# Fourier mixing and a gated convolution network on one Trainium2 core: a third product in the steps where VectorE has side work

## The chip, the cores and the metric

The kernel runs on one core of one Trainium2 chip. The metric is the device time of one execution in microseconds (us). The core's engines run side by side and meet at semaphores: TensorE (PE in the profile), VectorE (DVE), ScalarE (ACT), GpSimd (POOL), and SyncE (SP), whose queue issues most of the transfers.

## The reference

The input is `x`, 8 batches of 3136 x 256 in float32. It is Fourier-transformed along the sequence and the feature axis, and the real part goes into a gated network with 1024 hidden features:

```python
X = np.fft.fft(np.fft.fft(x, axis=1), axis=2).real
h = np.maximum(X @ w_in, 0.0)
conv_out = sum(conv_w[k] * hp[:, k:k + S, :] for k in range(3))   # hp: h padded by one row at each end
out = (h * (1.0 / (1.0 + np.exp(-conv_out)))) @ w_out
```

The code is condensed; the padding is along the sequence.

## The kernel before, in words

The transform along the sequence is done batch by batch. The rows of a batch are loaded as two halves `xh[b, 0]` and `xh[b, 1]`, the mirrored rows by four gathers each on GpSimd's queue (`load_ops`, L131). VectorE folds the rows onto each other: seven operations per half (`fold_ops`, L141 to L208: two `pair`, two `both`, `evens`, two `feats`), some 1.1 to 1.2 us each. TensorE multiplies the folded rows `w` by cosine and sine tables (`units`, PSUM tile `pd`), VectorE combines the parts into `pt` (cosine part) and `qt` (sine part). The feature transform is multiplied into `w_in` beforehand and gives the constant `G`, also of two halves.

The network then goes through 256 steps: 8 batches x 4 chunks of the half sequence x 8 blocks of 128 hidden features. A step computes the hidden rows at position k and at the mirrored position S-k together. Let a be the cosine product (PSUM tile `pa`, first filled by ScalarE's `seed`) and b the sine product (PSUM tile `pb`). The front half of the hidden rows is relu(a + b), the back half relu(a - b). In a step:

- `products` (L680): two fp32 matmuls, `pb` and `pa`; each is two instructions in the profile.
- `copies` (L687): ScalarE copies `pb` into `nb` twice, once with its sign changed (L693).
- `combine` (L695): VectorE adds `pa` and a half of `nb` and clamps at zero, once for the front and once for the back of `h` (L702). It asks for a buffer of `h` first (`row_of`, L674; 4 buffers), where GpSimd zeroes the two end columns in the first chunk of each batch (L678).
- `first_tap` (ScalarE, L707) and `tap` 1 and 2 (VectorE, L712): the convolution with three taps, over 770 or 832 columns.
- `sigmoid` (ScalarE, L725, in two pieces) and `gate`: the multiplication by `h`, half of the columns on GpSimd (L732) and half on VectorE (L733); in a batch's last chunk 64 more columns on GpSimd (L735).
- `mm2` (L737): the product with `w_out`, six tiles of 128 rows into `po`, accumulated over the 8 feature blocks.

The order of the instructions is written out by hand and each engine takes its queue in order. Cycle t of the main loop (L900) issues sigmoid(t-2), products(t+1), copies(t+1), combine(t), seed(t+2), first_tap(t), tap 1 and tap 2 of t-1, gate(t-2) and mm2(t-3). Side work is hung into cycles through the table `side`, under the names "first", "act", "dve", "pool", "load" and "pe". "dve" stands between the two taps. Side work in early cycles: the narrowing of the weights (`shared`: the last of w_in in cycle 0, w_out in cycles 2, 3, 5 and 7; L543 to L561), the feature column of all batches (`Feature`: `place` in cycle 5, L418 to L431, a VectorE stage in cycles 15 and 32), and the fold of batch 1 in cycles 9 to 19, with two operations in cycles 9, 12 and 16. The fold of batch 2 lies in cycles 20 to 35, and the products of batch 1's transform (`units`) in cycles 20 to 29. The transform of a batch runs through the steps of the batch before it.

Of the kernel before, what the change touches and what calls it, by code (L numbers as in the profile page):

```python
# [12 lines left out]
AF = mybir.ActivationFunctionType  # L13
# [19 lines left out]
BIG = 3.4028234663852886e38  # L33
# [3 lines left out]
def kernel(  # L37
# [10 lines left out]
    nc = tc.nc  # L48
    B, S, D = x.shape
    F = moe_w_in.shape[1]  # L50
    P = 128
# [9 lines left out]
    NF = F // P  # L61
# [27 lines left out]
    act = nc.scalar.activation  # L89

    def mm(o, l, r, start, stop):
        nc.tensor.matmul(o, l, r, start=start, stop=stop, skip_group_check=True)  # L92
# [16 lines left out]
    def load_ops(b, h, eng, other=None, held=False):  # L109


        def plain():
            t = xp.tile([P, 8, 2, D], F32, name="xh", tag="xh")
            xh[b, h] = t
            if held:

                nc.gpsimd.memset(t[0:1, 0, 0, 0:1], 0.0)
            eng.dma_start(out=t[0:NP, 0:4], in_=bass.AP(
                tensor=x.tensor, offset=x.offset + (b * S + 1 + 2 * h) * D,
                ap=[[HQ * D, NP], [Q4 * D, 4], [1, 2 * D]]))  # L120

        def zero():
            t = xh[b, h]
            for s0, n, r in ((0, 4, 0), (4, 3, 1), (7, 1, 0)):
                (other or eng).dma_start(out=t[NP:KR, s0:s0 + n], in_=bass.AP(
                    tensor=x.tensor, offset=x.offset + (b * S + r * Q4) * D,
                    ap=[[D, 1], [Q4 * D, n], [0, 2], [1, D]]))

        def mirrored(m):
            def f():  # L130
                nc.gpsimd.indirect_dma_start(  # L131
                    out=xh[b, h][0:NP, 7 - m].rearrange("p q d -> p (q d)"),
                    out_offset=None,
                    in_=bass.AP(tensor=x.tensor, offset=x.offset,
                                ap=[[2 * D, B * S // 2], [1, 2 * D]]),
                    in_offset=bass.IndirectOffsetOnAxis(ap=idx[0:NP, 0:1], axis=0),
                    element_offset=(b * S + (4 - m) * Q4 - HO + 2 * (1 - h)) * D)
            return f
        return [plain] + [zero] * h + [mirrored(m) for m in range(4)]
# [73 lines left out]
    PQ, eb, er = {}, {}, {}  # L213
# [416 lines left out]
    G = const.tile([P, 2, F], F32, name="G")  # L630
# [29 lines left out]
    hs, gs, pa, pb, po, nb = {}, {}, {}, {}, {}, {}  # L660

    def cut(s):
        b, c, f = s
        ch = chunks[c]
        return ch, ch.k1 - ch.k0, slice(f * P, (f + 1) * P)

    def seed(s):
# [3 lines left out]
        pa[s] = psa.tile([P, 512], F32, name="pa", tag="pa")  # L671
        act(pa[s][:, 0:n], eb[b, c], AF.Copy, scale=ge[:, f:f + 1])  # L672

    def row_of(s):  # L674
        hs[s] = hp.tile([P, HW], F32, name="h", tag="h")
        w = chunks[s[1]].w
        if chunks[s[1]].zeros:
            nc.gpsimd.memset(hs[s][:, 0:w:w - 1], 0.0)  # L678

    def products(s):  # L680
        b, c, f = s
        ch, n, fs = cut(s)
        pb[s] = psb.tile([P, 512], F32, name="pb", tag="pb")
        mm(pb[s][:, 0:n], G[0:P - 1, 1, fs], PQ[b][1][0:P - 1, ch.k0:ch.k1], True, True)
        mm(pa[s][:, 0:n], G[:, 0, fs], PQ[b][0][:, ch.k0:ch.k1], False, True)

    def copies(s):  # L687

        ch, n, fs = cut(s)
        p = pb.pop(s)  # L690
        nb[s] = nbp.tile([P, 2, HN], F32, name="nb", tag="nb")
        for i, cols in enumerate((ch.fcols, ch.cols)):
            act(nb[s][:, i, cols], p[:, cols], AF.Copy, scale=-1.0 if i else 1.0)  # L693

    def combine(s):  # L695

        ch, n, fs = cut(s)
        a, c = pa.pop(s), nb.pop(s)
        row_of(s)
        h = hs[s]  # L700
        for i, (to, cols) in enumerate(((h[:, ch.front], ch.fcols), (h[:, ch.back][:, ::-1], ch.cols))):
            nc.vector._custom_dve(TENSOR_ADD_SAT, out=to, in0=a[:, cols], in1=c[:, i, cols], s0=BIG, s1=0.0)  # L702

    def first_tap(s):
        n = chunks[s[1]].w - 2
# [7 lines left out]

    def shares(s):

        ch = chunks[s[1]]
        w = ch.w - 2
        n = ch.rest[0] if ch.last else w
        return slice(0, n // 2), slice(n // 2, n), slice(n, w)

    def sigmoid(s):

        v, p, r = shares(s)
        for c in (slice(p.start, r.stop), v):
            act(gs[s][:, c], gs[s][:, c], AF.Sigmoid)  # L725

    def gate(s):

        b, c, f = s
        g, h = gs[s], hs.pop(s)[:, 1:]  # L730
        v, p, r = shares(s)
        gt(g[:, p], g[:, p], h[:, p], op=ALU.mult)  # L732
        vt(g[:, v], g[:, v], h[:, v], op=ALU.mult)  # L733
        if r.start < r.stop:
            gt(left[:, f, b % 2 * LEFT:(b % 2 + 1) * LEFT], g[:, r], h[:, r], op=ALU.mult)  # L735
# [69 lines left out]
    n = chunks[0].k1  # L805
    p = psd.tile([P, 512], F32, name="pd", tag="pd")
# [8 lines left out]
    steps = [(b, c, f) for b in range(B) for c in range(len(chunks)) for f in range(NF)]  # L815
    per = len(chunks) * NF
    side = {}

    def at(cycle, where, fn):
        side.setdefault((cycle, where), []).append(fn)  # L820
# [6 lines left out]
    def shared(cycle, w, c):  # L827
        for where, fn in zip(("first", "dve"), w.parts(c, c + 2, room)):
            at(cycle, where, fn)

    shared(0, w_in[3], 0)
    for cycle, c in ((2, 0), (3, 2), (5, 4), (7, 6)):
        shared(cycle, w_out, c)
    for j, fn in enumerate(load_ops(1, 1, nc.sync)):
        at(NF + 1 + j // 3, "load", fn)

    ends = [9, 20, per + 4] + [per * (b - 1) - 3 for b in range(3, B)]
    taken = set()  # L840

    def free(cycle):

        while cycle in taken:
            cycle += 1
        taken.add(cycle)
        return cycle
# [13 lines left out]
    for b in range(1, B):  # L861
        begin, us, *_ = units(b)
        us = us[0:4] + us[5:]
        c0, n = ends[b], per * b - 3 - ends[b]
        at(max(c0, per * (b - 1) + 1), "pe", begin)
        cs = [c0 + i * n // len(us) for i in range(len(us) + 1)]
# [10 lines left out]
    for b in range(1, B):  # L877
        ops, singles = fold_ops(b)
        c0, n = ends[b - 1], ends[b] - ends[b - 1]
        cs = [free(c0 + j * n // len(ops)) if b > 1 else c0 + j * n // len(ops) for j in range(len(ops))]  # L880
        assert cs[-1] < ends[b] and (b > 1 or cs[7] > NF + 3)
        if b + 1 < B:
            for h in range(2):
                for j, fn in enumerate(load_ops(b + 1, h, nc.sync)):
                    at(cs[7 * h + 6] + 1 + j, "load", fn)
        for j, fn in enumerate(ops):
            at(cs[j], "dve", fn)
        for j, fn in singles.items():
            at(cs[j], "pool", fn)
# [4 lines left out]
    n = len(steps)  # L894
    seed(steps[0])
    seed(steps[1])
    products(steps[0])
    copies(steps[0])
    column(1)
    for t in range(n + LAG):  # L900
        def run(where):
            for fn in side.get((t, where), []):
                fn()
        if 0 <= t - 2 < n:
            sigmoid(steps[t - 2])
        run("first")
        if t + 1 < n:
            products(steps[t + 1])
            copies(steps[t + 1])
        run("act")  # L910
        if t < n:
            combine(steps[t])
        if t + 2 < n:
            seed(steps[t + 2])
        if t < n:
            first_tap(steps[t])

        if 0 <= t - 1 < n:
            tap(steps[t - 1], 1)
        run("dve")  # L920
        if 0 <= t - 1 < n:
            tap(steps[t - 1], 2)
        if 0 <= t - 2 < n:
            gate(steps[t - 2])
        run("pool")
        run("load")
        if t >= LAG:
            mm2(steps[t - LAG])
        run("pe")
# [66 lines left out]
```

## Time and profile before

The median of three runs is 1196.29 us (1195.91 to 1196.37).

| engine | busy us | share of the 1195.3 us span |
|---|---|---|
| TensorE (PE) | 1156.0 | 97% |
| VectorE (DVE) | 1135.0 | 95% |
| ScalarE (ACT) | 878.4 | 73% |
| GpSimd (POOL) | 477.5 | 40% |

The chain that ended last, which follows each instruction back to what released it, is 86% TensorE, 5% VectorE and 3% GpSimd. The share of all matmul time that goes to `po` is the largest (706.9 us), the taps (L712) are VectorE's largest group (580.1 us).

How to read the profile: a group's line gives its source line, engine, operation, output and inputs, the count, then busy time and the mean of one, then the time that the engine sat idle just before these instructions and what ended it. A line of the waits says who waited for whom, for how many us in total, how often, and the longest one. A line of the timeline gives the start in us, the length, the instruction, and in brackets the idle time before it. Neighbouring instructions of an engine overlap by about 0.1 us, so the distance from start to start is what one costs.

### The profile page before, as it was taken

The numbers are of one execution on the slowest core, as the hardware profiler recorded it, in microseconds if no ns is written. First come the engines' busy times: TensorE is split into PE (matmuls) and PEld (weight loads), VectorE is DVE, ScalarE is ACT, GpSimd is POOL, SyncE is SP. The second block draws the span as 40 slices with busy tenths as digits, with TensorE's granted clock in tenths as the row PEclk, the third lists the DMA queues.
The fourth block names the chain that finished last, engine by engine and source line by source line (L and its number), as shares of the span: only waits on it lengthen the run. The fifth ranks groups of instructions, "written<-read, shape, count | busy, mean of one in ns | idle before, by whom it ended". The sixth has DMA issues, their size and how long they took to land.

```text
span 1195.3 us, 15307 instructions
## 1 busy us (share of the span) xinstructions
PE 1156.0 (97%) x4802; PEld 888.5 (74%) x4802; DVE 1135.0 (95%) x1642; ACT 878.4 (73%) x1824; POOL 477.5 (40%) x540
## 2 busy tenths in 40 slices
PE   4988999999999999999999999999999999999998
PEld 2655677678777777777777777777777777777776
DVE  7899999999999999999999999999998998999996
ACT  2577666677777877777777777787776777788884
POOL 5225646454273342624345243632224232442224
PEclk9899999999999999999999999999999999999999
DMA  9802243211031210202021020310000100110000
GB/s 231 187 8 82 80 50 103 68 54 61 21 95 45 68 41 22 87 27 81 27 86 53 14 68 27 95 41 27 27 23 32 32 27 27 47 34 28 27 27 31
DMA packets 70067, 66.07 MB, mean 55 GB/s; under 512 B 28107, under 2 KB 57683, under 8 KB 69987
## 3 DMA queue, kind: packets, MB, share of 16 engines
q1 hardware_dynamic: 64349, 51.98, 15.3%
q0 software_dynamic: 5120, 12.85, 3.6%
q8 instruction: 38, 0.62, 0.2%
q10 hardware_dynamic: 518, 0.28, 0.1%
q14 instruction: 42, 0.34, 0.1%
HBM read 39.33 MB, written 25.74 MB: 54 GB/s over the span
## 4 chain that ended last, share of the span: by engine, by line
PE 86%; DVE 5%; issue 3%; POOL 3%; ACT 2%; DMA 0%; ACTq 0%; POOLq 0%; DVEq 0%; SPq 0%
PE po L92 53%; PE pb L92 13%; PE pa L92 13%; PE pd L92 7%; DVE g L712 2%; POOL xh L131 1%; DVE h L702 1%; DVE g L733 1%; ACT nb L693 0%; ACT os L752 0%; ACT g L725 0%; POOL left L735 0%; POOL g L732 0%; DVE w L194 0%; ACT pa L672 0%
## 5 line engine op out<-in xcount | busy, mean ns | idle before, releaser
L92 PE MATMUL po<-wout,g 128*128 128x256 f32 x3072 | 706.9, 380 | 16.8 <-DVE g L733 16.7
L92 PEld LDWEIGHTS po<-wout,g 128*128 128x128 f32 x3072 | 580.3, 190 | 164.2 <-DVE g L733 31.2
L712 DVE SCALAR_TENSOR_TENSOR g<-h,cw,g 128x770 f32<-128x770 f32 (+1 forms) x512 | 580.1, 1133 | 6.2 <-ACT g L707 2.2
L732 POOL TENSOR_TENSOR g<-g,h 128x385 f32<-128x385 f32 (+1 forms) x256 | 276.2, 1079 | 673.0 <-ACT g L725 471.1
L693 ACT ACTIVATE nb<-pb 128x386 f32<-128x386 f32 (+3 forms) x512 | 227.3, 498 | 183.9 <-PE pb L92 183.5
L725 ACT ACTIVATE g<-g 128x385 f32<-128x385 f32 (+2 forms) x512 | 244.3, 529 | 82.9 <-DVE g L712 82.0
L702 DVE CUSTOM_DVE_ANT_0 h<-pa,nb 128x386 f32<-128x386 f32 (+3 forms) x512 | 264.1, 556 | 7.4 <-POOL h L678 6.5
L707 ACT ACTIVATE g<-h,cw 128x770 f32<-128x770 f32 (+1 forms) x256 | 243.9, 953 | 0.0
L92 PE MATMUL pb<-qt,G 127*128 127x387 f32 (+2 forms) x512 | 214.4, 500 | 0.9 <-ACT G L641 0.9
L92 PE MATMUL pa<-pt,G 128*128 128x387 f32 (+2 forms) x512 | 211.8, 494 | 0.0
L672 ACT ACTIVATE pa<-eb,ge 128x387 f32<-128x387 f32 (+2 forms) x256 | 154.2, 603 | 2.5 <-DVE h L702 1.9
L92 PEld LDWEIGHTS pa<-pt,G 128*128 128x128 f32 x512 | 97.1, 190 | 73.8 <-issue 19.1
L733 DVE TENSOR_TENSOR g<-g,h 128x385 f32<-128x385 f32 (+1 forms) x256 | 147.4, 576 | 2.2 <-ACT g L725 2.2
L92 PE MATMUL pd<-tab,w 98*128 98x196 f32 (+3 forms) x448 | 118.4, 356 | 0.0
L131 POOL DMA_INDIRECT xh<-in_x_dram,idx x64 | 106.9, 1671 | 13.3 <-issue 10.8
L92 PEld LDWEIGHTS pb<-qt,G 127*128 127x128 f32 x512 | 91.2, 190 | 19.3 <-ACT G L641 2.0
L92 PEld LDWEIGHTS pd<-tab,w 98*128 98x128 f32 (+1 forms) x448 | 83.7, 191 | 12.3
L735 POOL TENSOR_TENSOR left<-g,h 128x64 f32<-128x64 f32 x64 | 63.8, 997 | 0.0
L752 ACT COPY os<-po 128x256 f32<-128x256 f32 x196 | 57.5, 389 | 8.0 <-PE po L92 4.7
L156 DVE TENSOR_TENSOR xh<-xh 98x1020 f32<-98x1020 f32 (+1 forms) x32 | 39.4, 1237 | 2.9 <-DMA xh<-in_x_dram,idx 2.9
L167 DVE TENSOR_TENSOR xh<-xh 98x1024 f32<-98x1024 f32 (+1 forms) x32 | 38.9, 1216 | 0.1
L178 POOL COPY w<-xh 98x4 f32<-98x4 f32 (+1 forms) x32 | 20.6, 644 | 6.1 <-DVE xh L167 3.6
(120 smaller groups left out, 316.5 us busy)
## 6 DMA issues: line engine op xcount, KB each, us to landing
out_dram<-os SPq DMA_DIRECT2D x192, 128.0 KB
xh<-in_x_dram SPq DMA_DIRECT2D x16, 784.0 KB
eb<-ed SPq DMA_DIRECT2D x16, 193.5 KB
tab<-dft_seq_dram SPq DMA_DIRECT2D x4, 589.5 KB
raw<-in_moe_w_in_dram SPq DMA_DIRECT2D x4, 512.0 KB
raw<-in_moe_w_out_dram SPq DMA_DIRECT2D x1, 2048.0 KB
eb<-ed SPq DMA_DIRECT2D x8, 209.0 KB
eb<-ed SPq DMA_DIRECT2D x7, 193.0 KB
```

What stands on the lines that cost most here:

```text
L92: nc.tensor.matmul(o, l, r, start=start, stop=stop, skip_group_check=True)
L131: nc.gpsimd.indirect_dma_start(out=xh[b, h][0:NP, 7 - m].rearrange("p q d -> p (q d)"), out_offset=None, in_=bass.AP(tensor=x.tensor, offs ...
L672: act(pa[s][:, 0:n], eb[b, c], AF.Copy, scale=ge[:, f:f + 1])
L693: act(nb[s][:, i, cols], p[:, cols], AF.Copy, scale=-1.0 if i else 1.0)
L702: nc.vector._custom_dve(TENSOR_ADD_SAT, out=to, in0=a[:, cols], in1=c[:, i, cols], s0=BIG, s1=0.0)
L707: act(gs[s], hs[s][:, 0:n], AF.Copy, scale=cw[:, 0, s[2]:s[2] + 1])
L712: stt(out=g, in0=h[:, k:k + n], scalar=cw[:, k, f:f + 1], in1=g, op0=ALU.mult, op1=ALU.add)
L725: act(gs[s][:, c], gs[s][:, c], AF.Sigmoid)
L732: gt(g[:, p], g[:, p], h[:, p], op=ALU.mult)
L733: vt(g[:, v], g[:, v], h[:, v], op=ALU.mult)
L735: gt(left[:, f, b % 2 * LEFT:(b % 2 + 1) * LEFT], g[:, r], h[:, r], op=ALU.mult)
L752: nc.scalar.copy(out=osb[:, j % 2], in_=pt[:, j % 2])
```

## The change

The change adds a third matmul to a step in which VectorE has side work: `pa` also accumulates the sine product, so it holds a + b, and ScalarE writes the front half of `h` as Relu of `pa` in place of a copy. The back half is still made by VectorE, from `pa` and -2b, since (a + b) - 2b = a - b. VectorE is left with one combine of the two. The test is `third(i)`: steps 3 to 19 and 30 to 35 with an entry under "dve". In a cycle with such a step the gate under way is split anew: three quarters on VectorE and a quarter on GpSimd. `row_of` is called a cycle earlier for these steps, in `copies`. Batch 1's fold starts in cycle 4 and has one operation in each cycle that is not taken by narrowing or the feature stage: cycles 4, 6, 8 to 14 and 16 to 20. The four gathers of batch 1's second half are issued one a cycle, in cycles 9 to 12, and not one in cycle 9 and three in cycle 10. The purpose is to take load off VectorE in these cycles and to make it even.

```diff
+    def triple(s):
+        return third(steps.index(s))
+
+    def third(i):
+        return (3 <= i < ends[1] or per - 2 <= i < ends[2]) and (i, "dve") in side
...
-        mm(pa[s][:, 0:n], G[:, 0, fs], PQ[b][0][:, ch.k0:ch.k1], False, True)
+        mm(pa[s][:, 0:n], G[:, 0, fs], PQ[b][0][:, ch.k0:ch.k1], False, not triple(s))
+        if triple(s):
+            mm(pa[s][:, 0:n], G[0:P - 1, 1, fs], PQ[b][1][0:P - 1, ch.k0:ch.k1], False, True)
...
-        for i, cols in enumerate((ch.fcols, ch.cols)):
-            act(nb[s][:, i, cols], p[:, cols], AF.Copy, scale=-1.0 if i else 1.0)
+        if triple(s):
+            act(nb[s][:, 1, ch.cols], p[:, ch.cols], AF.Copy, scale=-2.0)
+            row_of(s)
+            act(hs[s][:, ch.front], pa[s][:, ch.fcols], AF.Relu)
+        else:
+            for i, cols in enumerate((ch.fcols, ch.cols)):
+                act(nb[s][:, i, cols], p[:, cols], AF.Copy, scale=-1.0 if i else 1.0)
...
-        row_of(s)
+        if not triple(s):
+            row_of(s)
...
-            nc.vector._custom_dve(TENSOR_ADD_SAT, out=to, in0=a[:, cols], in1=c[:, i, cols], s0=BIG, s1=0.0)
+            if i or not triple(s):
+                nc.vector._custom_dve(TENSOR_ADD_SAT, out=to, in0=a[:, cols], in1=c[:, i, cols],
+                                      s0=BIG, s1=0.0)
...
-        return slice(0, n // 2), slice(n // 2, n), slice(n, w)
+        m = n - n // (4 if third(steps.index(s) + 2) else 2)
+        return slice(0, m), slice(m, n), slice(n, w)
...
-        at(NF + 1 + j // 3, "load", fn)
+        at(NF + 1 + max(j - 2, 0), "load", fn)
...
-        cs = [free(c0 + j * n // len(ops)) if b > 1 else c0 + j * n // len(ops) for j in range(len(ops))]
+        if b == 1:
+            cs = [c for c in range(4, ends[1] + 1) if c not in taken]
+            assert len(cs) == len(ops) and cs[7] > NF + 4
+        else:
+            cs = [free(c0 + j * n // len(ops)) for j in range(len(ops))]
```

The cycles of the w_out narrowing are entered in `taken` as well, so that the fold leaves them out.

More of the change, by code (lines that the diff above doesn't have):

```diff
@@ L817 @@
     side = {}
+    taken = set()
     def at(cycle, where, fn):
@@ L833 @@
         shared(cycle, w_out, c)
+        taken.add(cycle)
     for j, fn in enumerate(load_ops(1, 1, nc.sync)):
-        at(NF + 1 + j // 3, "load", fn)
+        at(NF + 1 + max(j - 2, 0), "load", fn)
     ends = [9, 20, per + 4] + [per * (b - 1) - 3 for b in range(3, B)]
-    taken = set()
     def free(cycle):
@@ L879 @@
         c0, n = ends[b - 1], ends[b] - ends[b - 1]
-        cs = [free(c0 + j * n // len(ops)) if b > 1 else c0 + j * n // len(ops) for j in range(len(ops))]
-        assert cs[-1] < ends[b] and (b > 1 or cs[7] > NF + 3)
+        if b == 1:
[3 more added lines that the diff above has]
+            cs = [free(c0 + j * n // len(ops)) for j in range(len(ops))]
+            assert cs[-1] < ends[b]
         if b + 1 < B:
```

## The prediction

> **What bounds the kernel now.** I read the page first: engines, groups, then the waits, then busy time by stretch. Engines and three groups:
>
> ```profile
> PE 1156.0 (97%) x4802; PEld 888.5 (74%) x4802; DVE 1135.0 (95%) x1642; ACT 878.4 (73%) x1824; POOL 477.5 (40%) x540
> ...
> L92 PE MATMUL po<-wout,g 128*128 128x256 f32 x3072 | 706.9, 380 | 16.8 <-DVE g L733 16.7
> L732 POOL TENSOR_TENSOR g<-g,h 128x385 f32<-128x385 f32 (+1 forms) x256 | 276.2, 1079 | 673.0 <-ACT g L725 471.1
> L702 DVE CUSTOM_DVE_ANT_0 h<-pa,nb 128x386 f32<-128x386 f32 (+3 forms) x512 | 264.1, 556 | 7.4 <-POOL h L678 6.5
> ```
>
> TensorE and VectorE are nearly equally loaded. TensorE waits in the step loop only for VectorE's gate (L733), 16.7 us in all. Which cycles? The waits between 63.75 and 150 us put nearly all of it there:
>
> ```profile
> PE po L92 <- DVE g L733: 13.9, 15, 2.8
> ```
>
> The same view for 196 to 246 us has 2.8 us in five waits. Busy time by stretch, cut where VectorE starts cycles 3, 9, 20, 30 and 36 (columns: stretch, length, then busy time and instructions of PE, PEld, DVE, ACT, POOL):
>
> ```profile
> 63.94:93.15 29.21, 23.63 (x94) 17.44 (x94) 27.70 (x47) 19.95 (x40) 6.57 (x17) 1.00 0.13 35
> 93.15:149.75 56.60, 48.75 (x193) 33.93 (x191) 56.53 (x81) 39.44 (x100) 33.07 (x25) 1.00 0.23 72
> 149.75:202.62 52.87, 52.59 (x224) 40.53 (x224) 52.06 (x82) 34.70 (x71) 24.71 (x27) 1.00 0.43 85
> 202.62:232.44 29.82, 27.35 (x112) 19.20 (x112) 28.77 (x41) 20.60 (x44) 18.84 (x21) 1.00 0.15 43
> ```
>
> Cycles 3 to 19 and 30 to 35 are bound by VectorE, the rest by TensorE. Only there can the change gain, and there it adds TensorE work.
>
> Last, VectorE's timeline in cycle 12 and GpSimd's near 146 us:
>
> ```profile
> 107.19 0.55 DVE L733 TENSOR_TENSOR g<-g,h 128x385 f32<-128x385 f32 x1
> 107.66 1.02 DVE L702 CUSTOM_DVE_ANT_0 h<-pa,nb 128x386 f32<-128x386 f32 x2
> 108.59 2.70 DVE L712 SCALAR_TENSOR_TENSOR g<-h,cw,g 128x770 f32<-128x770 f32 x1
> 111.22 1.21 DVE L167 TENSOR_TENSOR xh<-xh 98x1024 f32<-98x1024 f32 x1
> ```
>
> ```profile
> 146.30 4.25 POOL L732 TENSOR_TENSOR g<-g,h 128x385 f32<-128x385 f32 x1 [2.67 <-issue]
> ```
>
> A tap normally takes 1.01 us; here it took 2.70, while GpSimd, released by a long gather, ran two gate multiplies. The other way round, a GpSimd gate of 0.87 us took 4.25 and ended in the next combine pair. The two engines hold each other up except while VectorE runs the combine (L702)[...].
>
> [...] The trace shows 0.65 us from one product to the next for 387 columns in two recorded matmuls[...]. [...]
>
> **The change, part by part.** Durations are start to start in the timeline, since neighbours overlap.
>
> 1. The third product: 23 steps (3 to 19 and 30 to 35; every one of these cycles has VectorE side work) get one more matmul, 0.65 us each (0.71 for the two of 418 columns). 21 x 0.65 + 2 x 0.71 = 15.1 us on TensorE. A step without it is 2.59 (six tiles) + 2 x 0.65 = 3.89; with it 4.54.
> 2. VectorE loses one of two combines, 0.47, and takes 3/4 instead of 1/2 of the gate, +0.20: 0.27 less a step. A plain cycle is 0.93 (two combines) + 2 x 0.93 (taps) + 0.47 = 3.27; it becomes 3.00.
> 3. ScalarE: one copy becomes a Relu of the same shape and source (mean 0.50 us): nothing, as ScalarE is busy for 39.4 of 56.6 us in cycles 9 to 19. The Relu adds a wait for the third product and for the zeroing of `h`. Behind it stand seed(t+2), first_tap(t) and the next sigmoid; tap 1 waits for first_tap. With TensorE bound, the gate so delayed is ready about 3.5 us before its matmuls (Relu 0.5, seed 0.5, first tap 0.85, then 0.93 + 1.2 + 0.93 + 0.67 on VectorE, against two steps, 9.1). Hidden.
> 4. The gate's quarter on GpSimd: not in the trace. From L732 (385 in 0.87) and L735 (64 in 0.30) 192 elements take about 0.53 us. The combine window it fits in shrinks from 0.93 to 0.47. Bounds on the delay of VectorE's tap: 0 and 0.5 a cycle; I take 0.1.
> 5. The fold spread from cycle 4: moves work. Cycles 4, 6, 8 gain an operation, 9 and 12 lose their double, cycle 20 gets a second. Input for batch 1's first half was issued by 46 us and the transfers are quiet after 58, so a start near 70 us waits for nothing.
> 6. Gathers apart: one per cycle at 9 to 12. The last is needed in cycle 14; it lands about 3.9 us (median) after issue. A wait of up to 2 us would lie in VectorE's slack.
> 7. `h` is now zeroed before the other GpSimd work of a cycle, so the waits of the combine for L678 in cycles 6 (1.20 us) and 32 (1.05 us) go.
>
> Cycles 3 to 8. VectorE: six plain cycles 6 x 3.00 = 18.0; narrowing of w_out 3 x 2.40 + 2 x 0.33 = 7.9; fold 1.13 + 1.22 + 1.14 = 3.5; L420 0.16; sum 29.5, against 29.2 now. TensorE needs 6 x 4.54 = 27.2, so VectorE still binds and nothing is gained. Its gate for step 5 then ends near 89.3 us, and TensorE's matmuls of step 6 start at 89.3 + 2.69 + 1.95 = 93.95, now 93.86.
>
> Cycles 9 to 19. VectorE: 11 x 3.00 + ten fold operations 11.8 + the feature stage 0.83 = 45.6. TensorE up to step 17's matmuls: 11 x 3.89 + 9 x 0.65 + feature matmuls 2.0 = 50.7, and it becomes the bound. Now this takes 149.88 - 93.86 = 56.0. Gain 5.3.
>
> Cycle 20 has two fold operations (VectorE 5.6), but VectorE enters it some 2.9 us ahead, and the stretch to 202 us stays TensorE's.
>
> Cycles 30 to 35. TensorE gets 4 x 0.65 + 2 x 0.71 = 4.0 more; VectorE falls to 29.8 - 1.05 - 6 x 0.27 = 27.1, so TensorE binds and its idle time goes: 2.8 in the waits, with the starts after them (2.69 instead of 2.59 and the modelled ends) about 3.4. Loss 0.6.
>
> Sum: -5.3 + 0.6 + 0.5 (0.1 a cycle of locking in 3 to 8, where VectorE binds) = -4.2, so 1192.1 us.
>
> **Rivals.** (B) The lock eats it: VectorE stays the bound in 9 to 19. It lost 56.6 - 53.3 = 3.3 us to locks there (its operations sum to 11 x 3.27 + 16.5 + 0.83 = 53.3). Were that doubled because the window is halved: 45.6 + 6.6 = 52.2, 1.5 over TensorE; with 0.9 more in 3 to 8, 0.6 in 30 to 35 and 1.1 for late GpSimd quarters, the gain is 5.3 - 1.5 - 0.9 - 0.6 - 1.1 = 1.2: 1195.1. For it: the 4.25 and 2.70 us. Against: quarters are shorter, and a bound TensorE leaves VectorE gaps in which GpSimd gets through.
> (C) Slower: the third products cost in full and the waits shrink only by half, because the ScalarE chain behind the Relu holds the gates up. 13.8 (those behind cycle 3's first matmuls) + 0.5 for a later start - half of 18.0 + 3.4 = 3.6: 1199.9. For it: 15 us are added to the fuller engine to save 23 x 0.27 = 6.2 on the other. Against: the slack of part 3.
> (D) More: no locking in cycles 3 to 8 and the second stretch neutral: -5.4, so 1190.9.
>
> **How the numbers follow.** Main 0.64, D 0.08, B 0.18, C 0.10. Main and D are faster by over 2.4 us (0.2%), and so is 0.04 of B: faster 0.76; the rest of B is the same: 0.14; C slower: 0.10. Range 1190.0 to 1196.0: from D with 0.9 to spare, through B with locking at its upper bound, leaving C out.
>
> **What would show it.** TensorE's waits for VectorE's gate between 94 and 150 us nearly gone, and ScalarE waiting there for TensorE instead; step 17's matmuls near 145 us; cycles 3 to 8 as long as before; VectorE's waits for the zeroing of `h` gone; the stretch of cycles 30 to 35 about 0.6 us longer. It is wrong if TensorE still waits several us for L733's successor or for GpSimd's quarter in cycles 9 to 19, or if taps behind the single combine grow by more than 0.1 us in cycles 3 to 8.

## The result and the profile after

The changed kernel took 1191.47 us (median of four runs, 1190.21 to 1193.48) against 1196.33 us for the kernel before: ratio 0.9961, 95% interval 0.9943 to 0.9978. It is faster by 4.9 us; the forecast was 4.2.

The page of the changed kernel, engines and the groups that answer to those shown of before (L752 is the gate on GpSimd, L719 the combine, L753 the gate on VectorE):

```profile
PE 1163.0 (98%) x4848; PEld 896.1 (75%) x4848; DVE 1127.9 (95%) x1619; ACT 879.9 (74%) x1824; POOL 483.1 (41%) x540
...
L92 PE MATMUL po<-wout,g 128*128 128x256 f32 x3072 | 704.9, 379 | 2.3 <-DVE g L753 2.3
...
L752 POOL TENSOR_TENSOR g<-g,h 128x385 f32<-128x385 f32 (+2 forms) x256 | 274.2, 1071 | 647.3 <-ACT g L745 455.0
...
L719 DVE CUSTOM_DVE_ANT_0 h<-pa,nb 128x386 f32<-128x386 f32 (+2 forms) x489 | 253.6, 557 | 6.4 <-POOL h L686 4.9
```

TensorE has 46 more instructions (23 products of two each), VectorE 23 fewer. TensorE's waits for the gate fell from 16.7 to 2.3 us.

To place the gain I use the distance on TensorE's timeline between the first output matmuls of two steps. Four marks are enough: step 0 (cycle 3), step 6 (cycle 9), step 17 (cycle 20), and step 35 (cycle 38), after which both kernels run alike: from there to the end of the span it is 1195.3 - 241.45 = 953.85 us before and 1188.4 - 234.58 = 953.82 after. A step's products are issued just ahead of the output matmuls of the step four before it, so the first stretch also carries the third products of steps 9 and 10.

| stretch, us | before | changed | difference |
|---|---|---|---|
| step 0 to 6 | 30.11 | 30.44 | +0.33 |
| step 6 to 17 | 56.02 | 51.13 | -4.89 |
| step 17 to 35 | 91.57 | 91.25 | -0.32 |
| step 0 to 35 | 177.70 | 172.82 | -4.88 |

Busy time by stretch of the changed kernel, cut at the output matmuls of steps 0, 6, 17 and 27 and ending at those of step 35 (columns as before: length, then PE, PEld, DVE, ACT, POOL):

```profile
61.76:92.20 30.44, 28.17 (x109) 20.16 (x108) 30.23 (x45) 20.72 (x41) 7.32 (x19) 1.00 0.13 34
92.20:143.33 51.13, 51.13 (x210) 37.90 (x209) 49.03 (x64) 39.72 (x99) 33.35 (x23) 1.00 0.26 79
143.33:197.06 53.73, 53.73 (x229) 41.36 (x228) 52.85 (x82) 35.57 (x72) 28.59 (x28) 1.00 0.42 84
197.06:234.58 37.52, 37.52 (x158) 27.53 (x156) 35.24 (x47) 26.06 (x54) 23.75 (x24) 1.00 0.18 55
```

In the second, third and fourth line TensorE is busy without a gap; in the first VectorE is the bound still. The waits of the changed kernel between 92 and 144 us show who waits now (L703 is the copy of `pb`, L705 the Relu):

```profile
ACT nb L703 <- PE pb L92: 4.1, 4, 2.0
...
ACT h L705 <- PE pa L92: 2.6, 3, 0.9
...
DVE g L730 <- ACT g L725: 1.6, 3, 0.8
```

TensorE is in no line of this stretch as the one that waits for a gate. ScalarE waits for TensorE, and VectorE for ScalarE, as it must be where TensorE sets the pace.

### The profile page after: what moved, and what is told of

Read it like the earlier page. It is cut to its first block, busy times and chain, and to the rows that moved or that the text cites. A ratio compares the mean times of both kernels' runs of the same rounds, so it can differ in the third digit from the quotient of the medians.

```text
span 1188.4 us, 15358 instructions
## 1 busy us (share of the span) xinstructions
PE 1163.0 (98%) x4848; PEld 896.1 (75%) x4848; DVE 1127.9 (95%) x1619; ACT 879.9 (74%) x1824; POOL 483.1 (41%) x540
## 4 chain that ended last, share of the span: by engine, by line
PE 92%; DVE 3%; ACT 1%; issue 0%; DMA 0%; SPq 0%; ACTq 0%; DVEq 0%
PE po L92 56%; PE pa L92 15%; PE pb L92 14%; PE pd L92 8%; DVE g L730 1%; DVE g L753 0%; DVE raw L558 0%; DVE wout L551 0%; DVE h L719 0%; DMA out_dram<-os 0%; DVE wout L561 0%; ACT L745 0%; DVE xh L156 0%; DVE left L557 0%; DVE wout L543 0%
## 5 line engine op out<-in xcount | busy, mean ns | idle before, releaser
L752 POOL TENSOR_TENSOR g<-g,h 128x385 f32<-128x385 f32 (+2 forms) x256 | 274.2, 1071 | 647.3 <-ACT g L745 455.0
L708 ACT ACTIVATE nb<-pb 128x386 f32<-128x386 f32 (+2 forms) x466 | 207.5, 500 | 181.5 <-PE pb L92 181.0
L745 ACT ACTIVATE g<-g 128x385 f32<-128x385 f32 (+5 forms) x512 | 244.4, 530 | 61.5 <-DVE g L730 58.5
L719 DVE CUSTOM_DVE_ANT_0 h<-pa,nb 128x386 f32<-128x386 f32 (+2 forms) x489 | 253.6, 557 | 6.4 <-POOL h L686 4.9
L753 DVE TENSOR_TENSOR g<-g,h 128x385 f32<-128x385 f32 (+3 forms) x256 | 152.2, 594 | 2.2 <-ACT g L745 2.2
L131 POOL DMA_INDIRECT xh<-in_x_dram,idx x64 | 110.7, 1729 | 13.2 <-issue 10.9
L755 POOL TENSOR_TENSOR left<-g,h 128x64 f32<-128x64 f32 x64 | 67.1, 1048 | 0.0
```

Of the source, the lines that this page charges most:

```text
L131: nc.gpsimd.indirect_dma_start(out=xh[b, h][0:NP, 7 - m].rearrange("p q d -> p (q d)"), out_offset=None, in_=bass.AP(tensor=x.tensor, offs ...
```

## The experiments

All diffs are against the changed kernel. Ratios are to the kernel before on the same chip. The traces are compared from step 0 to step 35, as above: this distance of one kernel hardly varies (172.82 and 172.84 us in two traces of the changed kernel), while the whole time varies by some 3 us through the start (last section).

| kernel | 0 to 6 | 6 to 17 | 17 to 35 | 0 to 35, us | ratio (95%) |
|---|---|---|---|---|---|
| before | 30.11 | 56.02 | 91.57 | 177.70 | 1 |
| gathers alone (e5) | 30.13 | 54.54 | 91.56 | 176.23 | 0.9990 (0.9984 to 0.9997) |
| fold alone (e6) | 32.64 | 50.20 | 92.43 | 175.27 | 0.9982 (0.9975 to 0.9989) |
| fold and gathers (e2) | 32.65 | 48.86 | 92.44 | 173.95 | 0.9963 (0.9949 to 0.9976) |
| third products alone (e3) | 30.48 | 52.92 | 91.28 | 174.68 | 0.9976 (0.9967 to 0.9985) |
| changed | 30.44 | 51.13 | 91.25 | 172.82 | 0.9961 (0.9943 to 0.9978) |
| third in 3 to 8 only (e8) | 29.81 | 48.88 | 92.43 | 171.12 | 0.9951 (0.9939 to 0.9964) |

**Without third products (e2).**

```diff
-        return (3 <= i < ends[1] or per - 2 <= i < ends[2]) and (i, "dve") in side
+        return False
```

> The changed kernel without any third product or quarter gate: only the fold spread from cycle 4 and the gathers apart. Theory: VectorE stays the bound in cycles 3 to 19 with the same sum of work (about 31.5 to 32.7 us in cycles 3 to 8, about 51.7 in 9 to 19) and has a second fold operation in cycle 20, so the gain is small: ratio 0.9990 to 1.0004; the combine's wait of about 1.2 us for the zeroing of h in cycle 6 is back. Rival (the even spread of the fold is what brings the gain): 0.9965 or less.

The theory failed and the rival came out: fold and gathers alone give 0.9963, 3.75 of the 4.88 us in the trace. Cycles 3 to 8 took 32.65 us, within the expected range, with the wait for the zeroing back (1.2 us). But cycles 9 to 19 took 48.9 and not 51.7. VectorE's operations sum there to 11 x 3.27 + 11.8 + 0.83 = 48.6, so the 3.3 us that the prediction booked as locking are gone. (Locking, or the lock, stands in the recorded texts for VectorE and GpSimd holding each other up, as in the tap of 2.70 us for 1.01 and the gate of 4.25 us for 0.87 in the trace of before.) These 3.3 us are not all of the 7.16 us by which this stretch is shorter than before: about 4.7 are the four fold operations that moved out of it (16.5 - 11.8), and the stretches around it, where these now lie, became longer by 2.54 and 0.87. GpSimd's timeline of this kernel and, after it, VectorE's combines beside the second gate show how the two engines meet without it:

```profile
95.27 0.87 POOL L752 TENSOR_TENSOR g<-g,h 128x385 f32<-128x385 f32 x1 [3.57 <-issue]
...
97.23 1.24 POOL L131 DMA_INDIRECT xh<-in_x_dram,idx  x1 [0.19 <-issue]
99.73 0.86 POOL L752 TENSOR_TENSOR g<-g,h 128x385 f32<-128x385 f32 x1 [1.26 <-ACT g L745]
100.78 1.52 POOL L131 DMA_INDIRECT xh<-in_x_dram,idx  x1 [0.19 <-issue]
104.29 0.86 POOL L752 TENSOR_TENSOR g<-g,h 128x385 f32<-128x385 f32 x1 [2.00 <-ACT g L745]
105.34 1.51 POOL L131 DMA_INDIRECT xh<-in_x_dram,idx  x1 [0.18 <-issue]
```

```profile
99.47 1.01 DVE L719 CUSTOM_DVE_ANT_0 h<-pa,nb 128x386 f32<-128x386 f32 x2
```

Each of these cycles has one gate of 0.86 us, which lies in the window of the two combines (0.93 us) but for its last 0.1 to 0.2 us, and one gather of 1.2 to 1.5 us behind it. Nothing piles up, and between steps 6 and 17 no tap is drawn out by more than 0.15 us.

**The two parts of that, each alone (e5, e6).** The first has no third product and the old places of the fold, the second no third product and the old places of the gathers:

```diff
 # gathers alone, e5
-            cs = [c for c in range(4, ends[1] + 1) if c not in taken]
+            cs = [c0 + j * n // len(ops) for j in range(len(ops))]
 # fold alone, e6
-        at(NF + 1 + max(j - 2, 0), "load", fn)
+        at(NF + 1 + j // 3, "load", fn)
```

> The kernel before with only the gathers apart (one a cycle in 9 to 12); fold as before, no third product. Measured from TensorE's output matmuls of step 0 to those of step 35 (177.7 us before, 174.0 with fold and gathers). Theory L (three gathers in one cycle push GpSimd's gates out of the combine's window, and VectorE then stands still at the lock): the 2.70 us tap of cycle 12 becomes 1.0, and 176.0 or less. Theory F (the double fold cycles do it): 177.3 or more.

> The kernel before with only the fold of batch 1 spread from cycle 4, one operation a cycle; gathers as before (three in cycle 10), no third product. Theory L: the locking around the three gathers remains, so of the 3.7 us that fold and gathers together gain at most 2.2 are left: 175.5 us or more from step 0 to step 35. Theory F: the gain is the fold's: 174.3 or less.

Both count: 1.47 us and 2.43 us, in sum 3.9 against 3.75 together. Neither theory came out whole: the gathers alone miss theory L's bound by 0.23, and the fold alone, at 175.27, lies between the two, 0.23 under the bound of L and 0.97 over that of F. The tap of 2.70 us in cycle 12 is gone with the gathers apart, as theory L had it; what remains of long taps there is one of 1.78 us at 134.0. With the fold alone it is the reverse. GpSimd's timeline of e6 and, after it, VectorE's tap in the same place:

```profile
103.36 2.20 POOL L131 DMA_INDIRECT xh<-in_x_dram,idx  x1 [0.30 <-issue]
105.86 4.16 POOL L131 DMA_INDIRECT xh<-in_x_dram,idx  x1 [0.31 <-ACT nb L708]
110.06 1.69 POOL L752 TENSOR_TENSOR g<-g,h 128x385 f32<-128x385 f32 x2
```

```profile
110.04 2.54 DVE L730 SCALAR_TENSOR_TENSOR g<-h,cw,g 128x770 f32<-128x770 f32 x1
```

The second and third gather in a row take 2.2 and 4.2 us, GpSimd misses the window, two gates are late and run together, and VectorE's tap waits behind both: 1.5 us lost. What made the gathers themselves so long, no run separates.

**Third products alone (e3).** Both edits of e5 and e6, with third products:

> The third products and the quarter gate alone: the fold of batch 1 and the gathers lie as in the kernel before, so cycles 4, 6 and 8 have no third product and cycles 9, 12 and 16 have two fold operations. Theory: cycles 3 to 8 gain 2.0 us (three combines of 0.27 net, and the wait of 1.2 for the zeroing of h), cycles 9 to 19 need 50.3 us of VectorE plus about 3.3 of locking against 50.7 of TensorE, a gain of 2.4; less 0.4 in cycles 30 to 35: ratio about 0.9967. Rival (without the even spread the gain is lost to double cycles): 0.999 or more.

3.02 us in the trace, ratio 0.9976: between theory and rival. Cycles 3 to 8 gained nothing (30.48): the expectation had overlooked that step 6 has no third product when cycle 6 has no fold, so the combine there waits for the zeroing (1.2 us) as before, and that the stretch carries the third product of step 10 (0.65 us); two more waits of the combine (0.26 and 0.17 us, in cycles 4 and 8) took most of the rest. Cycles 9 to 19 gained 3.1, more than the 2.4 expected.

So each half of the change gives most of the gain without the other: 3.02 us and 3.75 apart, 4.88 together.

**The price of a third product (e9).**

```diff
+        return 3 <= i < ends[2] and (i, "dve") in side
```

> The changed kernel with third products (and the quarter gate) in steps 20 to 29 as well, where TensorE was the bound already: the price of the third product by itself. Theory: ten more at 0.65 to 0.71 us land in full, step 0 to step 35 takes 172.8 + 6.9 = 179.7 us, 59.3 of it from step 17 to 27 (53.7 with the change). Rival (part of a third product hides in TensorE's gaps): 177 us or less.

One execution was traced: 179.54 us from step 0 to step 35 and 59.31 from step 17 to step 27. The ten third products cost 6.72 us, so the price of 0.65 to 0.71 us lands in full where TensorE is the bound.

**Third products in cycles 3 to 8 only (e8).**

```diff
+        return 3 <= i < 9
```

> The changed kernel with third products and the quarter gate in steps 3 to 8 only. Theory: 30.4 us from step 0 to 6, 48.9 to step 17, then as without third products: 171.7 us from step 0 to step 35, ratio 0.9945 to 0.9955, better than the changed kernel. Rival: cycles 9 to 19 need the third product: 173 us or more.

As expected, 171.12 us, 1.7 shorter than the changed kernel. In cycles 9 to 19 the nine third products make TensorE the bound at 51.1 us, where VectorE without them is done in 48.9. In 3 to 8 they gain 32.65 - 29.81 = 2.8, and the first stretch is 0.6 shorter than expected, since steps 9 and 10 have no third product here. In time it is 1190.43 us (ratio in the table), and its interval overlaps that of the changed kernel; that it is faster is shown by the traces, not by the times.

**No third products in 30 to 35 (e1).**

```diff
+        return 3 <= i < ends[1] and (i, "dve") in side
```

> The changed kernel with third products in steps 3 to 19 only, none in 30 to 35 (there the gate is split in halves again). Theory (TensorE becomes the bound in cycles 9 to 19, and the second stretch pays about what it gains): the ratio to the kernel before stays within 0.0006 of the changed kernel's 0.9961, and TensorE's way from step 17's to step 35's output matmuls is 91.2 to 91.9 us (91.57 before, 91.25 with the change). Rival (the second stretch brings a good part of the gain): ratio 0.998 or more.

Ratio 0.9957 (0.9943 to 0.9970), 91.44 us from step 17 to step 35: the second stretch is worth 0.2 us. The theory holds. These 91.44 us are 1.0 less than without any third product (e2), though no third product lies behind step 17 here: relieved in cycles 9 to 19, VectorE starts cycle 20 1.32 us ahead of step 17's output matmuls, and 0.13 in e2.

**Half the gate on GpSimd everywhere (e4).**

```diff
-        m = n - n // (4 if third(steps.index(s) + 2) else 2)
+        m = n - n // 2
```

> The changed kernel with the gate split in halves everywhere, so GpSimd's piece is 0.87 us in a combine window of 0.47 us. Theory: in cycles 3 to 8 VectorE saves 0.2 us a cycle and loses about 0.3 to the lock, in 9 to 19 TensorE is the bound and hides either; ratio 0.9960 to 0.9968. Rival (the lock between VectorE and GpSimd decides in these cycles): GpSimd's halves come late, TensorE waits for them, ratio 0.998 or more.

Ratio 0.9964 (0.9951 to 0.9978), 173.80 us in the trace, 1.0 longer than with the quarter, 0.6 of it after step 17. The ratio is as the theory had it. VectorE's timeline of this kernel near 108 us:

```profile
107.85 0.67 DVE L193 TENSOR_TENSOR w<-xh 98x508 f32<-98x508 f32 x1
108.45 1.82 DVE L194 TENSOR_TENSOR w<-xh 98x508 f32<-98x508 f32 x1
```

The second of two equal operations takes 1.82 us in place of 0.68, while GpSimd's gate runs. I added up what the taps and fold operations between steps 6 and 17 lasted beyond their usual 1.01, 1.20, 1.21 and 0.68 us (only where it was over 0.06), and the mean of the eight gathers there:

| kernel | VectorE's overrun, us | mean gather, us |
|---|---|---|
| before | 3.02 | 2.08 |
| gathers alone (e5) | 1.49 | 1.62 |
| fold alone (e6) | 1.53 | 1.86 |
| fold and gathers (e2) | 0.15 | 1.41 |
| third in 3 to 8 only (e8) | 0.21 | 1.44 |
| changed | 2.35 | 2.84 |
| changed, half the gate (e4) | 5.48 | 1.56 |

So with the same fold and gathers the third products bring the overrun back (5.48 us with half the gate, 0.15 without third products), and the quarter gate more than halves it (2.35). That the single combine is too narrow a window is how I read the timelines. In the changed kernel a gather keeps GpSimd past the window, and VectorE's next fold operation (usually 1.21 us) runs beside the late gate:

```profile
92.37 4.36 POOL L131 DMA_INDIRECT xh<-in_x_dram,idx  x1 [0.18 <-issue]
96.76 1.01 POOL L752 TENSOR_TENSOR g<-g,h 128x192 f32<-128x192 f32 x1
```

```profile
95.74 0.55 DVE L719 CUSTOM_DVE_ANT_0 h<-pa,nb 128x386 f32<-128x386 f32 x1
96.21 1.18 DVE L730 SCALAR_TENSOR_TENSOR g<-h,cw,g 128x770 f32<-128x770 f32 x1
97.31 1.54 DVE L167 TENSOR_TENSOR xh<-xh 98x1024 f32<-98x1024 f32 x1
```

TensorE, busy without a gap there, hides it.

**A mix, and two tries at more (e7, e10, e11).** e7 has third products in 3 to 8 and in every third cycle after:

```diff
+        return i in (3, 4, 5, 6, 7, 8, 10, 13, 16, 19, 31, 33, 35)
```

> The changed kernel with third products (and the quarter gate) only in steps 3 to 8, 10, 13, 16, 19, 31, 33 and 35. Theory (with the even fold VectorE needs only 48.9 us in cycles 9 to 19 without a third product, so nine of them at 0.65 us make TensorE the bound for nothing; in 3 to 8 TensorE is idle and they gain 2.2): step 0 to 35 takes 169 to 171 us, ratio 0.9925 to 0.9945. Rival (the third products carry the gain in 9 to 19 too): 173 us or more, ratio 0.9965 or more.

The theory failed: 173.22 us, on the rival's side, ratio 0.9961 (0.9948 to 0.9974), between the two; 51.49 from step 6 to step 17. GpSimd's timeline shows what a balance of sums leaves out:

```profile
124.76 4.50 POOL L752 TENSOR_TENSOR g<-g,h 128x192 f32<-128x192 f32 x1 [1.36 <-ACT g L745]
129.45 4.77 POOL L131 DMA_INDIRECT xh<-in_x_dram,idx  x1 [0.19 <-issue]
134.25 0.87 POOL L752 TENSOR_TENSOR g<-g,h 128x385 f32<-128x385 f32 x1
```

and VectorE then stood still for a buffer of `h` that this late gate still held:

```profile
135.15 1.03 DVE L719 CUSTOM_DVE_ANT_0 h<-pa,nb 128x386 f32<-128x386 f32 x2 [1.82 <-POOL g L752]
136.10 2.14 DVE L730 SCALAR_TENSOR_TENSOR g<-h,cw,g 128x770 f32<-128x770 f32 x1
```

A quarter gate missed its narrow window, all that GpSimd had to do after it came a cycle late, and VectorE, which had no slack here, paid twice: 1.82 us of waiting, and a tap of 2.14.

e10 and e11 keep cycle 20 free of batch 2's fold; e10 has third products in 3 to 8 only, e11 also in 30 to 35:

```diff
             assert len(cs) == len(ops) and cs[7] > NF + 4
+            taken.add(ends[1])
```

> Third products in steps 3 to 8 only, and cycle 20 kept free of batch 2's fold, which starts a cycle later. Theory (the second fold operation of cycle 20 costs VectorE 1 us that TensorE's bound does not hide here): 52.9 us from step 17 to step 27 in place of 53.7, 170.3 from step 0 to step 35. Rival (that loss comes from something else): 171.0 or more.

> Third products in steps 3 to 8 and 30 to 35, cycle 20 kept free of batch 2's fold. Theory: 37.5 to 38.0 us from step 27 to step 35 as in the changed kernel (38.7 without third products there), but up to 1.4 more before step 27 for two of them: 169.5 to 170.6 us from step 0 to step 35; ratio 0.9935 to 0.9950. Rival (no gain from the second stretch): 171 or more.

e10: 170.77 us, ratio 0.9957 (0.9944 to 0.9970); 53.40 from step 17 to step 27, 0.3 better than with the double fold and 0.5 short of the theory; where these 0.5 go stays open. e11: 171.46 us, ratio 0.9956 (0.9941 to 0.9970): in the trace the rival's side, the second stretch gains nothing. VectorE waited 2.05 us there for one Relu. The Relu itself had waited 4.83 us for GpSimd's zeroing of `h` (L686), which stood behind a multiplication over 64 columns (L755, undisturbed 0.30 us) that took 6.62:

```profile
204.11 6.62 POOL L755 TENSOR_TENSOR left<-g,h 128x64 f32<-128x64 f32 x1
210.93 1.01 POOL L131 DMA_INDIRECT xh<-in_x_dram,idx  x1 [0.19 <-issue]
211.94 0.12 POOL L686 MEMSET h<- 128x2 f32 x1
```

```profile
212.09 0.49 ACT L705 ACTIVATE h<-pa 128x385 f32<-128x385 f32 x1 [4.83 <-POOL h L686]
```

A late piece on GpSimd is paid for once more here: the third product makes ScalarE, and through it VectorE, depend on GpSimd's queue.

**The changed kernel again (e12).**

> The changed kernel once more, beside the two above. 172.8 us from step 0 to step 35, ratio 0.9950 to 0.9970, 1.5 to 3 us slower than third products in 3 to 8 alone.

172.84 us, 1192.21 us, ratio 0.9963 (0.9950 to 0.9976), on the same chip as e10 (1190.38) and e11 (1190.63). As expected, though single executions of the three overlap.

## Why the prediction was right, and where it was not

**TensorE becomes the bound in cycles 9 to 19.** Right. The stretch was to take 50.7 us and took 51.13; step 17's matmuls were to come near 145 us and came at 143.33, 2.0 us of it from an earlier start (63.75 and 61.76), so 145.3 on the clock of the kernel before.

**Cycles 3 to 8 gain nothing.** Right: 30.44 for 30.11. The hold-up was taken at 0.1 us a cycle, 0.5 in the sum; the trace has two fold operations drawn out by 0.34 and 0.37 us, and no tap. The combine's wait for the zeroing of `h` is gone in cycle 6, as part 7 said. In cycle 32 part 7 was wrong: there the Relu waits for the zeroing (2.87 us), and the combine waits 0.88 us for the Relu, where it had waited 1.05 for the zeroing.

**Price of a third product, 0.65 to 0.71 us.** Right, by e9 to 0.2 us in 6.9. So were the estimates of parts 2 and 4: VectorE's larger gate takes 0.67 us start to start (0.47 before), GpSimd's quarter 0.51 to 0.53 where nothing disturbs it. The trace of before gives part 2's 0.20 as an estimate too: its taps take 1.015 us for 770 columns and 1.084 for 832 (medians), 1.1 ns a column, so 0.21 us for the 193 columns that the gate gains.

**Cycles 20 to 35 lose 0.6.** The size was off, and over the whole stretch the sign. To step 32 it was a loss of 0.42; but the prediction stopped its sum there, and cycles 36 to 38, where TensorE had also stood behind VectorE (0.33 us of waiting at step 33), gained 0.73. The term is -0.32 in place of +0.6. Beside e1, which has no third product there, the second stretch costs 0.54 to step 32, close to the 0.6, and then brings 0.73. VectorE entered cycle 20 only 1.32 us ahead of step 17's matmuls (0.13 before), not some 2.9, but with that lead TensorE stayed busy.

**The sum.** +0.33 - 4.89 - 0.32 = -4.88 in the trace, and -4.9 in time, for -4.2.

**What the gain comes from.** Here a step of the working failed, though the sum did not show it: the sum compares the two kernels as wholes, and it was right that TensorE is the bound of the second. Parts 5 and 6 booked the fold's spread and the gathers apart as moved work, worth nothing, and 3.3 us of hold-up in cycles 9 to 19 as a cost that TensorE's new bound would cover. e2 shows that the two edits take the hold-up away by themselves (overrun 3.02 to 0.15 us) and give 3.75 us without any third product. The prediction's own durations point to it: without third products the spread leaves VectorE 48.6 us of work in cycles 9 to 19, hold-up apart, less than the 50.7 that TensorE was to need with them. On top of the two edits the third products add 1.13: -2.21 in cycles 3 to 8, +2.27 in 9 to 19, -1.19 after step 17, of which e1 has 1.0. In 9 to 19 they cost more than they bring, even with that 1.0, and the changed kernel is 1.7 us slower in the trace than with third products in 3 to 8 alone.

How VectorE and GpSimd meet can be counted over the whole trace of before: 208 of GpSimd's multiplications took at most 0.1 us more than the shortest of their form (0.85 us for 384 or 385 columns, 0.29 for 64). 69% of their time lies beside a combine, and no combine was drawn out by 0.1 us. Beside a tap within 0.1 us of its median none of them ran for more than 0.26 us; in the changed kernel the two figures are 69% and 0.30 us. The prediction used the hold-up to size a cost and did not ask what the change does to the order in which GpSimd meets VectorE.

**Rival B** was right that VectorE is held up with the single combine (overrun 2.35 us in the changed kernel, and e7 and e4 show gates that miss the window), wrong in its size (6.6 us) and in that the overrun does not reach the path while TensorE is the bound. **Rival C** fell: the chain behind the Relu held no gate up between 92 and 144 us; in e11 it held VectorE's combine up by 2.05 us. **Rival D** (its terms sum to -5.3, not -5.4) was right that the second stretch costs nothing and wrong on cycles 3 to 8; the -4.88 lie between it and the forecast.

## What to carry to other kernels

When one edit spreads load and another moves it to a different engine, price each against the schedule that the other leaves: evenly spread, VectorE's load in cycles 9 to 19 already fitted in 48.9 us, and moving part of it to TensorE made that engine the bound at 51.1. Where a trace shows two engines holding each other up, as VectorE's taps and GpSimd's gates do here (a tap of 2.54 us for 1.01 in e6), count the windows in which the second runs undisturbed, and keep its work to one window's worth per cycle; in e7 a late piece cost twice, 1.82 us of waiting for the buffer that it held and a tap of 2.14 us.

## What the runs showed of the hardware that I had not expected

A gather's length on GpSimd differed with its place: alone in its cycle behind a gate in the wide window it took 1.2 to 1.5 us, as the third in a row 4.15, and in the changed kernel, with a single combine as the window, up to 4.36. What lengthens it stays open.

The start of the kernel does not repeat. The granted TensorE clock between 40 and 50 us after the start was 0.66 in some traces, 0.83 or 1.00 in others, and the first output matmuls came at 63.1 to 64.6, 62.5 to 63.1 and 60.5 to 61.8 us. In the trace of before it is 0.50 from 41.61 to 48.44 us, 6.83 us long; a mean of 0.83 would be 3.4 us at 0.50, an estimate ((1 - 0.83) x 10 / 0.50). Two lines of the busy time by stretch, of the kernel before and of the changed one (the seventh number after the stretch is the clock):

```profile
40.00:50.00 10.00, 8.71 (x31) 6.09 (x29) 8.58 (x20) 3.25 (x8) 4.13 (x7) 0.66 0.77 251
```

```profile
40.00:50.00 10.00, 9.06 (x42) 6.47 (x42) 9.53 (x21) 5.60 (x14) 5.36 (x10) 1.00 0.74 250
```

It differs between traces of one kernel (1.00 and 0.66 in the two of the changed kernel), and goes with the 3 us by which runs of one kernel differ: the four runs of the changed kernel have mean clocks of 1.000, 0.998, 0.998 and 0.996 over the whole span and times of 1190.2, 1191.4, 1191.5 and 1193.5 us. What makes the clock drop is open.
